# A two-layer gated network behind a normalised attention: chunk 1's second layer by 26 products, transfers of x on one queue, new places for the interleaved steps

## The chip, the cores and the metric

The kernel runs on one core of a Trainium2 chip. The metric is the device time of one execution in microseconds; lower is better. "TensorE", "VectorE", "ScalarE", "GpSimd" and "SyncE" appear in the profile as PE (its weight loads as PEld), DVE, ACT, POOL and SP. A transfer that an engine's queue issues is written SPq, ACTq or POOLq.

## The reference

```python
# q, k, v: (8 batches, 8 heads, 576, 64) float32;  D = 512 = 8 heads x 64
kv  = einsum('bhsd,bhse->bhde', k, v)
out = einsum('bhsd,bhde->bhse', q, kv)
rms = sqrt(mean(out * out, axis=-1, keepdims=True) + 1e-6)
x   = (out / rms * g_norm).transpose(0, 2, 1, 3).reshape(4608, 512)
gate = 1 / (1 + exp(-(x @ w_gate)))      # w_gate, w_val: (512, 1536) float64 in memory
val  = x @ w_val
y    = (gate * val) @ w_out              # w_out: (1536, 512);  y: (4608, 512) float32
```

## The kernel before

The 4608 rows of x are worked in nine chunks of 512 tokens (c = 0 to 8). A chunk has a first layer (x times w_gate and w_val, sigmoid, product: the tensor called h) and a second layer (h times w_out). Batches of 576 rows do not line up with chunks, so x lives in a ring of three chunks (`xT_ring`, tile xT), which batch b+1 fills while chunk b is worked.

Chunk 0 is computed plainly while the weights are converted from float64. From chunk 1 on the first layer is done by a scheme that multiplies matrices cut in 4x2 and 2x4 blocks with 26 products of blocks instead of 32. It runs three times (j = 0, 1, 2, over a third of the hidden units each): 26 products of two 128x256 matmuls. `PRODUCTS1` lists them in order: a PSUM region, the sum of weight blocks, the sum of x blocks, and what is done once the product stands (copies by ScalarE, additions by VectorE, multiplications by GpSimd, sigmoids by ScalarE). The product number p = 26 j + i, 0 to 77, is the clock by which all other steps are placed. `second_layer_fast` does the second layer the same way, with 26 products of three 128x256 matmuls (`PRODUCTS2`). Only five PSUM banks serve the eleven regions: a bank is handed on when its last reader has been issued, so a late VectorE or ScalarE holds up TensorE.

The scheme needs sums of blocks, made by other engines:
- sums of w1 (both first-layer weights, tile w): made once by GpSimd (`w1_sums`, L740), used by chunk 1 where they lie, and stored to memory by SyncE (`keep_w1`, L757, 69 pieces, into kept1) so that chunks 2 to 8 can load them (`load_granule`, L769, on GpSimd's queue);
- sums of x (`x_sums`, 18 a chunk, L829 and L831) by VectorE, placed in the second layer of the chunk before;
- sums of h (`h_sums`, L721), by GpSimd and, for eight of them, by VectorE;
- sums of w_out (18, `W_SUMS`): made once, stored to kept3, and loaded by chunks 2 to 8 (`load_w`, L987).

Chunk 1's second layer is the exception before the change: `second_layer_plain` does it with 4 x 12 matmuls of 128x512, and meanwhile `w_forms` has VectorE make the 18 sums of w_out (L1007, L1009) and GpSimd's queue store them (L1010). Its keep stores of the third part of w1 and four loads of granules fall there too.

Chunks 1 to 6 also carry the attention of batch c + 1 (`feed`). Its steps are: `kv_mm` and four `kv_copies` (L366, L372, L377); two `turn`s for each pair of heads (a VectorE transpose of q, L383, and then the load of the next q by SyncE, L104); and for each two pairs `u_mm` (L407), a square on ScalarE (L413), two sums (L416), a root, two normalisations (L425) and two `x_turn`s. An x_turn has VectorE transpose the result (L432, tile xTs) and then issues the transfers that bring it into the ring (L442): four, or six where the ring wraps. For the first two pairs all are issued by SyncE. For the last two pairs (`two_pairs(n0 + 2, nc.scalar)`) half are issued by ScalarE.

The order of everything is written out by hand: the program runs through the products, and a table says after which product each step is issued. Each engine works its own queue strictly in order. `at1` holds the places in the first layer (p = 0 to 77), `at2` those in the second (0 to 47 matmuls when plain, 0 to 25 products when fast). The last two x_turns are placed at 4 and 8 of the plain layer, and at 4 and 5 of the fast ones. The x sums for the next chunk begin at 23 in the plain layer, at 14 in chunks 2 to 6 and at 6 in chunk 7.

Of the kernel before, what the change touches and what calls it, by code (L numbers as in the profile page):

```python
# [20 lines left out]
def kernel(  # L21
# [332 lines left out]
    def feed(b):  # L354
# [30 lines left out]
            if e == 1:  # L385
                load_q(n + 1)

        def two_pairs(n0, queue=nc.sync):


            d = {}
# [36 lines left out]
            def x_turn(i):  # L428


                for which in range(2):
                    nc.vector.transpose(xTs[:, i, which],  # L432
                                        sq.rearrange("p r (w g i c) -> p w i r g c", w=2, g=JH, i=NC)[:, which, i])
                m = n0 % NHP
                for j in range(2):
                    for e in range(2):
                        p0, p1 = HD * e + QB * j, HD * e + QB * i
                        s0 = 0
                        while s0 < S // 2:
                            o = (S * b + S // 2 * j + s0) % (NX * G)  # L440
                            n_ = min(NX * G - o, S // 2 - s0)
                            (nc.sync, queue)[j].dma_start(out=xT_ring[p1:p1 + QB, m:m + 2, o:o + n_],  # L442
                                                          in_=xTs[p0:p0 + QB, i, :, s0:s0 + n_])
                            s0 += n_

# [3 lines left out]
        def turns_of(n):  # L449
# [2 lines left out]
        n0 = NHP * b  # L452
        kv = [kv_mm] + [lambda i=i: kv_copies(i, range(3)) for i in range(2 * NC)]
        t0, t1, t2, t3 = (turns_of(n0 + i) for i in range(4))
        u0, u1 = two_pairs(n0), two_pairs(n0 + 2, nc.scalar)
        first = list(zip((1, 5, 14, 22, 27, 29, 30, 31, 32, 33, 37, 38, 46, 47, 49, 52, 53, 53, 55, 56, 57, 60, 61, 63),
                         t0 + t1 + u0[:1] + t2[:1] + u0[1:2] + t2[1:] + u0[2:5] + t3[:1] + u0[5:6] + t3[1:] + u0[6:] +
                         u1[:7]))
        return kv, first, u1[7:]

    def flush():
# [73 lines left out]
    def give(i):  # L535
        free.append(i)
# [374 lines left out]
    def first_layer_fast(c, at):  # L911
# [3 lines left out]
        for j in range(N3):  # L915
# [7 lines left out]
            for i, (name, hv, wv, steps) in enumerate(PRODUCTS1):  # L923
                part, p = next(n for n, r in enumerate(PARTS) if i in r), NPR * j + i
                new = name not in regions
                if new:
                    i_ = free.popleft()
                    regions[name] = i_, pair(bank(i_))
                ws = w1_form(c, j, part, hv)
                for g in range(2):  # L930
                    nc.tensor.matmul(regions[name][1][:, g], ws[:, g], xf[c][wv], start=(new and g == 0), stop=True,  # L931
                                     skip_group_check=True)
                combine(o, regions, steps, nc.vector if j == N3 - 1 and i == NPR - 1 else nc.gpsimd)
                give_all(regions, LAST1, i)
                for step in at.get(p, ()):
                    step()
                for _ in range(2 if i % HALF == HALF - 1 else 1):
                    if h_fill:
                        h_fill.popleft()[1]()
                if c > 1:  # L940
                    g_ = NPA * (N3 * (c - 2) + j) + part
                    if p < NPR * N3 - 1:
                        wait = (3 if part < 2 else 0) if j == 0 and c + 1 < B else 0
                        if wait and i == PARTS[part][-1]:
                            held[i + wait] = g_ + NPA
                        elif i == PARTS[part][-1]:
                            load_granule(g_ + NPA)
                        if j == 0 and i in held:
                            load_granule(held.pop(i))
                    k_, r = divmod(p - 20, 2)  # L950
                    if r == 0 and 0 <= k_ < NR:
                        load_w((c - 2) * NS + k_)
                else:
                    if p in (NPR, 2 * NPR):
                        keep_w1(j - 1)
                    if keeping:
                        keeping.popleft()()
                    if NPR <= p < NPR + len(W_ORDER) - W1_FIRST:
                        w1_sums(2, slice(W1_FIRST + p - NPR, W1_FIRST + p - NPR + 1))
                    if p == 2 * NPR + HALF:  # L960
                        load_granule(0)
                        load_granule(1)
            if c > 1:
                h_fill.extend(h_sums(j, slice(SUMS_FIRST) if j else slice(None)))

    tok = [slice(P * i, P * i + P) for i in range(NT)]

# [18 lines left out]
        if i < N_FAST * NS:  # L986
            nc.gpsimd.dma_start(out=ring(i), in_=kept3[i % NS].rearrange("p (j n) -> p j n", j=N3))  # L987

    def w_forms():

        last = {}
        for n, (_, _, x, _, y) in enumerate(W_SUMS):
            last[x] = last[y] = n
        more = h_more.rearrange("p j s c -> p (j s c)").rearrange("p (i j n) -> p i j n", j=N3, n=DH)
        spare = deque(w_ring + [more[:, i] for i in range(2 * N3)])
        at = {v: w_raw(v) for v in range(8)}
        steps = []
        for n, (v, sx_, x, sy, y) in enumerate(W_SUMS):
            at[v] = spare.popleft()
            for u in {x, y, v}:  # L1000
                if u > 7 and last.get(u, n) <= n:
                    spare.append(at[u])

            def make(v=v, sx_=sx_, x=x, sy=sy, y=y, o=at[v], a=at[x], b=at[y]):
                op = op_of(sy)
                if sx_ > 0:
                    tt(out=o, in0=a, in1=b, op=op)  # L1007
                else:
                    nc.vector.scalar_tensor_tensor(out=o, in0=a, scalar=-1.0, in1=b, op0=ALU.mult, op1=op)  # L1009
                nc.gpsimd.dma_start(out=kept3[STREAM.index(v)].rearrange("p (j n) -> p j n", j=N3), in_=o)  # L1010
            steps.append(make)
        return steps

    def second_layer_plain(c, at):
        keep_w1(N3 - 1)
        while keeping:
            keeping.popleft()()
        loads = {4: 2, 8: 3}
        order_ = [block(l, j) for j in range(N3) for l in (0, 2, 1, 3)]
        for t in range(NT):  # L1020
            i = free.popleft()
            ps = bank(i)
            for n, f in enumerate(order_):
                nc.tensor.matmul(ps, gv[c, f][:, tok[t]], w2[:, f, :], start=(n == 0), stop=(n == NFT - 1),
                                 skip_group_check=True)
                if NFT * t + n in loads:
                    load_granule(loads[NFT * t + n])
                for step in at.get(NFT * t + n, ()):
                    step()
            ot = sg_tile()  # L1030
            nc.scalar.copy(out=ot, in_=ps)
            give(i)
            store(c, t, ot)
        load_late(c + 2)

    def second_layer_fast(c, at):
        o = {f"t{n}": temps[:, i, 0:DH] for i, n in enumerate((0, 1, 8, 9))}
# [3 lines left out]
                o[f"o{2 * t + n}"] = rows[t][:, DH * n:DH * n + DH]  # L1041
        regions, used, done = {}, {}, count()
        ends = (nc.sync, nc.scalar) if c == NG - 1 else (nc.sync,)
        dones = {18: 0, 22: 1, 24: 2, 25: 3}

        def product(i, js):
            name, hv, wv, _ = PRODUCTS2[i]
            if i not in used:
                used[i] = name not in regions
                if used[i]:  # L1050
                    regions[name] = take()
            ws = w_raw(wv) if wv < 8 else ring((c - 2) * NS + STREAM.index(wv))
            for j in js:
                nc.tensor.matmul(regions[name][1], h_form(hv, j), ws[:, j], start=(used[i] and j == 0),  # L1054
                                 stop=(j == N3 - 1), skip_group_check=True)
# [1 line left out]
        def finish(i):  # L1057
            _, _, wv, steps = PRODUCTS2[i]
            combine(o, regions, steps, nc.gpsimd)
            give_all(regions, LAST2, i)  # L1060
            if wv > 7 and STREAM.index(wv) + NR < NS:
                load_w((c - 2) * NS + STREAM.index(wv) + NR)
            if i == 16:
                load_granule(NPA * N3 * (c - 1) + NPA - 1)
            if i in dones:
                t = dones[i]
# [50 lines left out]
        store(0, t, ot)  # L1117

    flush()
    for c in range(1, NG):  # L1120
        at1, at2 = {}, {}
        if c + 1 < B:
            kv, first_, then = second_batch if c == 1 else feed(c + 1)
            for p, step in (list(zip((17, 17, 19, 20, 22), kv)) if c > 1 else []) + first_:
                at1.setdefault(p, []).append(step)
            for p, step in zip((4, 8) if c == 1 else (4, 5), then):
                at2.setdefault(p, []).append(step)
        if c + 1 < NG:
            p0, two = (23, 18) if c == 1 else (14, 12) if c + 1 < B else (6, 0)
            p = p0  # L1130
            for n, step in enumerate(lambda n=n, c=c: x_sum(c + 1, n) for n in range(len(X_SUMS))):
                at2.setdefault(p, []).append(step)
                p += (2 if c == 1 else 1) if n % 2 or n >= two else 0
        if c == 1:
            for n, step in enumerate(w_forms()):
                at2.setdefault(2 * n, []).append(step)
        first_layer_fast(c, at1)
        if c == 1:
            sgs += [spare_sg] + more_sgs
        (second_layer_plain if c == 1 else second_layer_fast)(c, at2)  # L1140


# [28 lines left out]
```

## Time and profile before

| what | us |
|---|---|
| median of three runs (1031.4, 1031.47, 1035.5) | 1031.47 |
| profiled execution | 1032.79 |
| span of the profiled execution, first to last instruction | 1031.0 |
| TensorE matmul busy | 1016.1 |
| VectorE busy | 718.1 |
| GpSimd busy | 565.2 |
| ScalarE busy | 347.6 |
| chunk 1: first layer, second layer (plain) | 71.24, 41.20 |
| chunk 6: first layer, second layer (fast) | 74.09, 35.02 |
| chunk 7: first layer, second layer (fast, no batch fed) | 67.53, 33.68 |

The stages are cut where the matmuls change from one line to the other: L931 is the first layer's matmul, L1024 the plain second layer's, L1054 the fast second layer's, L407, L366 and L372 the attention's. A matmul of float32 shows as two records, so a chunk's first layer has 312 records, a fast second layer 156 and the plain one 96. In busy times the clock of TensorE is at its full value throughout (0.999 on average). A group's line gives the count, the busy time, the mean of one in nanoseconds, and the idle time in front of it with what ended that idle time.

### The profile page before, as it was taken

To read this page: it belongs to the slowest core of one execution; us is meant where nothing else is said; L and a number is where in the kernel's file an instruction comes from. 1 tells how busy PE (TensorE), PEld (TensorE's weight loads), DVE (VectorE), ACT (ScalarE), POOL (GpSimd) and SP (SyncE) were. 2 spreads that over 40 slices of the span, in tenths; PEclk is the share of its full clock that TensorE was granted. 3 is DMA by queue.
4 is the path that set the end of the run, shared out by engine and by line. 5 is a ranking of instruction groups with operands and counts; after the bars stand their busy time and mean duration, and the time that the engine had idled before them with its cause. 6 is when DMAs were issued, how large, how long until landed. Compare 5 with 4: busy or idle time off the path is not lost. (4 is left out here: it accounts for less than half of the span.)

```text
span 1031.0 us, 18177 instructions
## 1 busy us (share of the span) xinstructions
PE 1016.1 (99%) x6854; PEld 815.5 (79%) x6854; DVE 718.1 (70%) x1188; ACT 347.6 (34%) x604; POOL 565.2 (55%) x922
## 2 busy tenths in 40 slices
PE   9999999999999999999999999999999999999998
PEld 8644447884588888888888888888888888888887
DVE  4899899776558865786577566866588556755672
ACT  4654422440244304441254115421453033203320
POOL 0001999522149641967087716963396439753963
PEclk9999999999999999999999999999999999999999
DMA  9975311469977466846685567755774656454714
GB/s 263 271 248 171 123 41 53 147 194 305 348 239 251 159 189 221 302 158 194 193 301 179 179 190 254 243 154 170 240 252 159 183 164 240 158 164 154 252 61 121
DMA packets 102183, 203.31 MB, mean 197 GB/s; under 512 B 27792, under 2 KB 74128, under 8 KB 102096
## 3 DMA queue, kind: packets, MB, share of 16 engines
q0 software_dynamic: 24448, 128.20, 37.0%
q1 hardware_dynamic: 68240, 70.08, 23.0%
q10 hardware_dynamic: 9408, 3.87, 1.5%
q8 instruction: 54, 0.88, 0.4%
q14 instruction: 33, 0.27, 0.1%
HBM read 168.30 MB, written 26.74 MB: 189 GB/s over the span
## 5 line engine op out<-in xcount | busy, mean ns | idle before, releaser
L931 PE MATMUL mm<-xs,w 128*128 128x256 f32 x1428 | 334.2, 380 | 0.6 <-DVE h L901 0.4
L931 PEld LDWEIGHTS mm<-xs,w 128*128 128x128 f32 x1428 | 270.0, 190 | 40.7 <-DVE sg L901 1.5
L931 PE MATMUL mm<-xT,w 128*128 128x256 f32 x948 | 230.2, 380 | 0.0
L931 PEld LDWEIGHTS mm<-xT,w 128*128 128x128 f32 x948 | 179.1, 190 | 25.5 <-issue 1.0
L901 DVE TENSOR_TENSOR sg<-sg,mm 128x512 f32<-128x512 f32 (+1 forms) x169 | 98.6, 607 | 112.8 <-PE mm L931 56.8
L769 POOL DMA_DIRECT2D w<-kept x84 | 46.8, 557 | 207.7 <-PE mm L931 199.2
L1054 PE MATMUL mm<-w,h 128*128 128x256 f32 x558 | 126.6, 379 | 0.0
L897 ACT COPY temps<-mm 128x512 f32<-128x512 f32 (+1 forms) x124 | 64.8, 548 | 182.9 <-PE mm L931 92.6
L893 POOL TENSOR_TENSOR h<-h,sg 128x512 f32<-128x512 f32 x72 | 94.1, 1324 | 56.8 <-ACT sg L890 46.4
L1054 PEld LDWEIGHTS mm<-w,h 128*128 128x128 f32 x558 | 106.0, 190 | 14.4
L721 POOL TENSOR_TENSOR h<-h 128x128 f32<-128x128 f32 x189 | 95.3, 516 | 14.5 <-DVE h_more L721 11.4
L890 ACT ACTIVATE sg<-sg 128x512 f32<-128x512 f32 x96 | 59.8, 630 | 107.4 <-DVE sg L901 107.1
L1054 PE MATMUL mm<-w,h_more 128*128 128x256 f32 x390 | 90.1, 380 | 5.6 <-ACT temps L897 5.6
L1054 PEld LDWEIGHTS mm<-w,h_more 128*128 128x128 f32 x390 | 73.7, 190 | 17.5 <-ACT temps L897 7.7
L897 ACT COPY sg<-mm 128x512 f32<-128x512 f32 (+1 forms) x107 | 54.6, 521 | 80.7 <-PE mm L1054 42.7
L560 PE MATMUL mm<-xT,w 128*128 128x512 f32 x176 | 77.7, 594 | 0.0
L901 DVE TENSOR_TENSOR temps<-temps,mm 128x512 f32<-128x512 f32 (+1 forms) x93 | 58.2, 625 | 23.8 <-PE mm L1054 15.6
L901 DVE TENSOR_TENSOR temps<-mm,temps 128x512 f32<-128x512 f32 (+1 forms) x62 | 38.9, 627 | 50.1 <-PE mm L1054 22.5
L897 ACT COPY h<-mm 128x512 f32<-128x512 f32 x48 | 28.0, 585 | 121.9 <-PE mm L931 121.8
L721 POOL TENSOR_TENSOR h_more<-h 128x128 f32<-128x128 f32 x105 | 51.9, 497 | 30.7 <-DVE h L893 27.3
L740 POOL TENSOR_TENSOR h_more<-w 128x256 f32<-128x256 f32 x10 | 12.9, 1302 | 97.5 <-PE at L366 97.5
L987 POOL DMA_DIRECT2D w<-kept x102 | 62.8, 617 | 1.4 <-issue 1.0
(140 smaller groups left out, 1347.7 us busy)
## 6 DMA issues: line engine op xcount, KB each, us to landing
w<-kept POOLq DMA_DIRECT2D x102, 384.0 KB, 4.8
w<-kept POOLq DMA_DIRECT2D x42, 896.0 KB, 5.4
w<-kept POOLq DMA_DIRECT2D x42, 768.0 KB, 5.3
w_ring<-kept POOLq DMA_DIRECT2D x24, 384.0 KB, 5.0
q<-in_q_dram SPq DMA_DIRECT2D x24, 288.0 KB, 3.7
out_dram<-sg SPq DMA_DIRECT2D x104, 64.0 KB, 1.7
st<-in_moe_w_gate_dram SPq DMA_DIRECT2D x12, 512.0 KB, 5.4
st<-in_moe_w_val_dram SPq DMA_DIRECT2D x12, 512.0 KB, 6.7
```

The lines of the kernel that those rows point to most:

```text
L560: nc.tensor.matmul(self.ps[i], w[("wg", "wv")[i], self.f][:, m, :], xT[self.c][:, m, :], start=(m == 0), stop=(m == NMT - 1), skip_group_c ...
L721: ops.append((eng, lambda v=v, x=x, sign=sign, y=y, eng=eng: eng.tensor_tensor(out=h_form(v, j), in0=h_form(x, j), in1=h_form(y, j), op=op ...
L740: nc.gpsimd.tensor_tensor(out=w1_slot(j, w_at[v]), in0=w1_slot(j, w_at[x]), in1=w1_slot(j, w_at[y]), op=op_of(sign))
L769: nc.gpsimd.dma_start(out=granule(g)[:, 0:n], in_=kept1[g // NPA % N3, g % NPA][:, 0:n])
L890: nc.scalar.activation(out=o["o" + step[1]], in_=o["o" + step[1]], func=AF.Sigmoid)
L893: mult.tensor_tensor(out=o[x], in0=o[x], in1=o[y], op=ALU.mult)
L897: nc.scalar.copy(out=o[out_], in_=o[expr])
L901: tt(out=o[out_], in0=o[x], in1=o[y], op=ALU.add if sign == "+" else ALU.subtract)
L931: nc.tensor.matmul(regions[name][1][:, g], ws[:, g], xf[c][wv], start=(new and g == 0), stop=True, skip_group_check=True)
L987: nc.gpsimd.dma_start(out=ring(i), in_=kept3[i % NS].rearrange("p (j n) -> p j n", j=N3))
L1054: nc.tensor.matmul(regions[name][1], h_form(hv, j), ws[:, j], start=(used[i] and j == 0), stop=(j == N3 - 1), skip_group_check=True)
```

## The change

1. **Chunk 1's second layer** is done by `second_layer_fast` like the others; `second_layer_plain` and `w_forms` go. The 18 sums of w_out are made one by one by `w_form` (L999, L1001 in the new file): nine in chunk 1's first layer and nine in its second layer, each at a place in the table, 12 by VectorE and 6 by GpSimd (the number at the end of each triple says which: 1 is GpSimd). They lie in parts of w1 that are already used and stored (`w_place`, `W_AT`). Each is stored to kept3 by SyncE instead of GpSimd's queue.
2. **Keep stores of w1** start at p = 0 instead of 26, one after each product; those of the third part start at p = 39. The four granule loads for chunk 2 move to products 9, 10, 13 and 23 of the second layer. Sums of h are now made in chunk 1 too.
3. **All transfers of x** are issued by SyncE.
4. **Places**: the attention's steps, the k-by-v steps and the x sums get new places in chunks 1 to 7, as explicit lists, with one list for the steps of batch 2 (chunk 1) and one for the other batches.

The diff, cut to its core:

```diff
-        def two_pairs(n0, queue=nc.sync):
+        def two_pairs(n0):
...
-                            (nc.sync, queue)[j].dma_start(out=xT_ring[p1:p1 + QB, m:m + 2, o:o + n_],
+                            nc.sync.dma_start(out=xT_ring[p1:p1 + QB, m:m + 2, o:o + n_],
...
-        u0, u1 = two_pairs(n0), two_pairs(n0 + 2, nc.scalar)
-        first = list(zip((1, 5, 14, 22, 27, 29, 30, 31, 32, 33, 37, 38, 46, 47, 49, 52, 53, 53, 55, 56, 57, 60, 61, 63),
-                         t0 + t1 + u0[:1] + t2[:1] + u0[1:2] + t2[1:] + u0[2:5] + t3[:1] + u0[5:6] + t3[1:] + u0[6:] +
-                         u1[:7]))
+        u0, u1 = two_pairs(n0), two_pairs(n0 + 2)
+        steps_ = t0 + t1 + t2 + t3 + u0 + u1[:7]
+        first = [(p, steps_[i]) for p, i in (((4, 0), (5, 1), (8, 2), (21, 3), (25, 8), (28, 4), (28, 5), (29, 9), (30, 10), (31, 11), (32, 6), (42, 12), (48, 13), (48, 7), (50, 14), (53, 15), (53, 16), (53, 17), (56, 18), (57, 19), (57, 20), (60, 21), (60, 22), (65, 23)) if b == 2 else
+                                             ((3, 0), (7, 1), (24, 2), (24, 3), (28, 8), (28, 4), (30, 5), (30, 9), (32, 10), (32, 11), (37, 12), (39, 6), (45, 13), (47, 7), (47, 14), (53, 15), (53, 16), (54, 17), (56, 18), (56, 19), (56, 20), (60, 21), (61, 22), (63, 23)))]
...
-                    if p in (NPR, 2 * NPR):
-                        keep_w1(j - 1)
+                    if p == 0:
+                        keep_w1(0)
+                        keep_w1(1)
+                    elif p == NPR + HALF:
+                        keep_w1(2)
...
-                    if p == 2 * NPR + HALF:
-                        load_granule(0)
-                        load_granule(1)
-            if c > 1:
-                h_fill.extend(h_sums(j, slice(SUMS_FIRST) if j else slice(None)))
+            h_fill.extend(h_sums(j, slice(SUMS_FIRST) if j else slice(None)))
...
+    def w_place(at):
+        return w1_flat[:, at:at + N3 * DH].rearrange("p (j n) -> p j n", j=N3)
+
+    W_AT = {v: w_place(at) for v, at in {10: 0, 12: 768, 14: 1536, 9: 2304, 13: 3072, 16: 4096, 19: 4864, 11: 5632, 8: 6400}.items()}
+    W_AT.update((v, w_raw(v)) for v in range(8))
+    W_AT.update(zip((22, 20, 21, 17, 18, 25, 23), w_ring[:5] + w_ring[6:]))
+    W_AT.update(((24, w_raw(5)), (15, w_raw(0))))
+
+    def w_form(v, eng):
+        sx_, x, sy, y = next(s_[1:] for s_ in W_SUMS if s_[0] == v)
+        if sx_ > 0:
+            eng.tensor_tensor(out=W_AT[v], in0=W_AT[x], in1=W_AT[y], op=op_of(sy))
+        else:
+            nc.vector.scalar_tensor_tensor(out=W_AT[v], in0=W_AT[x], scalar=-1.0, in1=W_AT[y], op0=ALU.mult,
+                                           op1=op_of(sy))
+        nc.sync.dma_start(out=kept3[STREAM.index(v)].rearrange("p (j n) -> p j n", j=N3), in_=W_AT[v])
...
+        first_loads = {9: 0, 10: 1, 13: 2, 23: 3}
...
-            ws = w_raw(wv) if wv < 8 else ring((c - 2) * NS + STREAM.index(wv))
+            ws = W_AT[wv] if c == 1 else w_raw(wv) if wv < 8 else ring((c - 2) * NS + STREAM.index(wv))
...
+    X1 = (12, 15, 16, 18, 18, 18, 18, 19, 19, 20, 20, 21, 21, 22, 22, 23, 23, 23)
+    X2 = (14, 15, 16, 17, 19, 19, 22, 23, 24, 25, 25, 25, 25, 25, 25, 25, 25, 25)
+    X3 = (7, 8, 11, 11, 12, 13, 14, 14, 16, 16, 19, 22, 22, 22, 22, 23, 23, 23)
...
-            for p, step in (list(zip((17, 17, 19, 20, 22), kv)) if c > 1 else []) + first_:
+            for p, step in (list(zip((19, 19, 19, 24, 24), kv)) if c > 1 else []) + first_:
...
-            for p, step in zip((4, 8) if c == 1 else (4, 5), then):
+            for p, step in zip((4, 4) if c == 1 else (5, 5), then):
...
-            p0, two = (23, 18) if c == 1 else (14, 12) if c + 1 < B else (6, 0)
...
+            for n, p in enumerate(X1 if c == 1 else X2 if c + 1 < B else X3):
+                at2.setdefault(p, []).append(lambda n=n, c=c: x_sum(c + 1, n))
...
+            for at_, forms in ((at1, ((27, 9, 0), (28, 10, 0), (34, 12, 0), (52, 8, 1), (53, 13, 0), (56, 14, 0), (62, 11, 1), (71, 16, 1), (74, 19, 0))), (at2, ((0, 22, 0), (3, 23, 1), (4, 25, 1), (6, 21, 1), (8, 24, 0), (9, 15, 0), (10, 20, 0), (12, 17, 0), (12, 18, 0)))):
...
-        (second_layer_plain if c == 1 else second_layer_fast)(c, at2)
+        second_layer_fast(c, at2)
```

## The prediction

> **What bounds it now.** I read the page first, then the busy time by stage, the chain of waits, the waits in total and the timeline of one second layer.
>
> ```profile
> PE 1016.1 (99%) x6854; PEld 815.5 (79%) x6854; DVE 718.1 (70%) x1188; ACT 347.6 (34%) x604; POOL 565.2 (55%) x922
> L1024 PE MATMUL mm<-w,h 128*128 128x512 f32 x96 | 41.4, 592 | 0.0
> ```
>
> TensorE is never short of work for long, so only two things can shorten the kernel: fewer matmul columns, or the few stalls left. The stages from 162 us on (cut where the matmuls change line):
>
> ```profile
> 162.38:233.62 71.24, 71.24 (x601) 62.49 (x600) 55.94 (x89) 30.65 (x48) 39.39 (x45) 1.00 0.45 143
> 233.62:274.82 41.20, 41.20 (x97) 18.24 (x96) 27.51 (x47) 1.66 (x3) 10.88 (x20) 1.00 0.94 340
> ...
> 788.77:823.79 35.02, 33.93 (x157) 29.56 (x156) 23.21 (x56) 3.35 (x9) 18.88 (x39) 1.00 0.49 145
> ...
> 891.32:925.00 33.68, 33.68 (x158) 29.65 (x157) 23.20 (x53) 3.35 (x9) 20.17 (x39) 1.00 0.51 152
> ```
>
> Columns: length, then busy time of PE, PEld, DVE, ACT, POOL, then clock, DMA share, GB/s. Row 1 is chunk 1's first layer, row 2 its plain second layer (41.20 us, DMA at 340 GB/s), row 3 chunk 6's second layer by 26 products, row 4 the same for chunk 7, which feeds no batch. The work is 33.68 us; chunk 6 loses 1.34 us. The chain says where:
>
> ```profile
> 796.34 0.76 DVE xTs L432 x2
> 797.10 0.02 issue
> 797.12 0.64 ACTq L442
> 797.76 0.04 issue
> 797.80 0.82 ACTq L442
> 798.62 0.04 issue
> 798.66 0.38 ACT temps L897
> 799.04 0.04 issue
> 799.09 24.87 PE mm L1054 x114
> ```
>
> ScalarE stands in its queue behind two transfers of x (L442), which wait for VectorE's transposes (L432); the copy of product 4's sum (L897) comes late, and product 7, which accumulates into that bank, waits. Behind 799 the chain is TensorE alone. It recurs once in each of chunks 2 to 6:
>
> ```profile
> PE mm L1054 <- ACT temps L897: 5.6, 5, 1.3
> SPq L442 <- DMA xT<-xTs: 6.8, 4, 3.1
> ```
>
> Line 1: 5.6 us in five waits. Line 2: SyncE's transfers of x also wait for earlier ones to land (used below).
>
> [...] The trace agrees: SP and ACT issue L442 in 0.60 and 0.64 us, landing after 4.6 and 5.1 us. Moving the issue should cost SP's time alone. [...] The trace fits: the x sums (L829, 128x256) take 421 ns at the median and 950 ns at most, the long ones at 161 to 168 us beside GpSimd's L740. [...] GpSimd's rows agree: (1324 - 497) / 384 = 2.15 ns (L893 128x512 against L721 128x128).
>
> **Part 1: chunk 1's second layer.** Removed: 96 matmul records of 128x512, 41.20 us. Added: 26 products, 156 records, 33.68 us by chunk 7's row. TensorE's work: **-7.5 us**. The copies, combinations and sums of h that come with the 26 products are those of chunk 7's row (DVE 23.2, POOL 20.2, ACT 3.4 us busy), where they hide behind TensorE. What may stall it:
>
> (a) Sums of w_out. VectorE makes 12 (6 in each layer), GpSimd 6 (3 in each). VectorE's take 0.95 us each (L1007 rows): 5.7 us on top of 23.2 busy in a second layer of 33.7, so 29 of 34, and tight. GpSimd's 128x768 has no row: by the slope, 0.50 + 640 x 2.15 ns = 1.9 us; at worst three times L740's locked 1.42 us, 4.3 us; I take 1.9. GpSimd's sum 25 is needed soonest, by product 11, which starts 11 x 1.296 = 14.3 us into the layer. In chunk 6 GpSimd's first eight sums of h end near 8.4 us, 7.8 without the 0.6 us load issued between them; then sum 23, two of h, sum 25: 7.8 + 1.9 + 1.0 + 1.9 = 12.6 us. Hidden by 1.7 us at my price; at 4.3 us it would cost TensorE 3.1. The 18 stores of the sums leave GpSimd's queue (L1010, 0.54 us each, 9.8 us) for SP's; GpSimd is not the bound, so I count nothing for that.
>
> (b) x for chunk 2. The two transposing steps run behind VectorE's eight sums of h and form 22, at about 8.4 to 10 us. SP then issues 12 transfers, and ahead of them stands the store of GpSimd's sum 23 (ready at 9.7). SP and ACT have eight completion counters in rotation: a transfer waits for the one eight before. Twelve at 0.63 us from 10.2: the eleventh, the last chunk 2 needs, goes out at 16.5 us and lands after 3 us in quiet (first layer of chunk 1: 212.29 to 215.04) or 6 to 9 as in the old plain layer: 19.5 to 25. VectorE reaches its first x sum at about 18.2 us and stands in order, with two sums of w_out and the subtraction that frees product 18's bank behind it: 19.9 + 1.9 + 0.4 = 22.2 us against 23.3 needed; four operations later product 19's bank, 24.4 against 24.6. So there is next to no slack, and GpSimd's locks cost some. I charge **1.4 us** (0 to 5).
>
> (c) First layer of chunk 1 (0.1 us of stall visible now): six VectorE sums, 5.7 us over 56 of 71 busy, three by GpSimd (39 of 71 busy). Stores of w1 go out earlier, from product 0, one a product; each landed in 1.9 us, and the first sum placed over them comes five products behind the last. If the sum of product 52 on GpSimd is late, SP's queue with x behind it is late too, with some 3 us to spare. **+0.4 us** (0 to 2). The granule loads, now at products 9, 10, 13 and 23, are first read 20 us on: nothing, covered by the rest of the layer.
>
> **Part 2: transfers of x by SyncE.** In chunks 2 to 6 ACT no longer waits. The five second layers sum to 175.33 us; five times 33.68 is 168.4: 6.9 us to gain. What is late next: VectorE's o1=o1+B at 798.10 needs only to precede product 11, and GpSimd's sums end 5 us or more ahead of their products. SP issues 8 transfers instead of 4 (12 in the wrapped chunk): 797.12 + 7 x 0.63 = 801.5, landed by 807, against the first x sum at about 809. Hidden, with 2 us to spare; without that cover each late microsecond would stand in front of VectorE's combinations. Behind them on SP are only the stores of the output, 10 us later. I take **-6.5 us** (-7 to -3).
>
> **Part 3: places of steps.** First layers of chunks 2 to 6 sum to 373.6 us. Their work is 67.5 (chunk 7) + 5.9 (72-head block twice 1.78 and 1.73, k by v 2.41) + 0.3 for switching = 73.75; the excess is 4.9. Of it 1.2 us is a wait with no releaser (549.28), which no step touches. Visible causes: in chunk 3 VectorE held 3.86 us by a q load that the turn at product 14 reached too soon (0.57 us of TensorE), and k-by-v copies late for the matmul at product 27 (0.3). The new places (turns at 24, matmul at 28) clear both; copies on ACT now bunch at 24. **-1.0 us** (-2.5 to +2). The nine x sums put at product 25 run into the next first layer, where VectorE's first combination is due 6 us in; nine take 3.8: nothing, covered by that gap.
>
> **Sum.** -7.5 + 1.4 + 0.4 - 6.5 - 1.0 = **-13.2 us**. The profiled execution took 1032.79 us (span 1031.0, 1.8 around it), the median of the runs is 1031.47. Against the profiled one it gives 1019.6 (span near 1018); against the median, 1018.3, which I forecast.
>
> **Rivals.**
> 1. *The handover from chunk 1 becomes the wait.* SP has 18 stores of w_out and 69 of w1 in one queue with x. For: the old layer's x landed in 6 to 9 us, and (b) has no slack. Against: that was beside 340 GB/s, now spread. TensorE would lose 4 to 9 us there: 1022 to 1027.
> 2. *The ACT wait is replaced* in chunks 2 to 6 by one of similar size, for VectorE's bank releases or SP. For: PE comes 1.3 us earlier to VectorE. Against: VectorE idles 2.16 and 0.94 us right after. Part 2 then brings 0: 1024.8.
> 3. *Slower.* x by SyncE alone lands late in all of chunks 1 to 6: each x sum blocks VectorE, and TensorE stops for a bank. It decides once landing takes 2 us over chunk 6's 5; at 10 us each chunk loses 3 to 4: six give about 20, no 6.5 gain, less 7.5: about 1037. For: eight in flight at most. Against: 8 transfers need no second round, and nothing landed so late outside the saturated layer.
> 4. *It doesn't do what it says*: product 11 or others wait for their sums and chunk 1's layer stays near 41 us: 1024.
>
> **Numbers.** As forecast (1014.5 to 1022): 0.72. Rivals 1, 2 and 4 together 0.24, four fifths of it under 1026.3. Rival 3: 0.04. 0.5%, 5.2 us, is about what a measurement of this kernel can tell from no change: faster 0.89, same 0.07, slower 0.04. The range holds the forecast's own spread and the larger part of rivals 1, 2 and 4: 1014 to 1025.5.
>
> **What would show it.** Right: chunk 1's second layer at 34 to 36 us with 156 records of 128x256; the wait of L1054 on ACT gone and chunks 2 to 6 at 33.7 to 34.2; no L442 on ACT. Wrong: VectorE waiting for xT in the x sums (rival 1, 3), TensorE waiting for VectorE in L1054 (2), or for GpSimd's sums (4), or first layers of chunks 2 to 6 above 74.7 us on average.

## The result and the profile after

| | before | after |
|---|---|---|
| median of four runs each, us | 1031.93 (1031.4 to 1035.5) | 1020.83 (1019.7 to 1023.12) |
| profiled execution, its span | 1032.79, 1031.0 | 1021.93, 1020.1 |

The ratio is 0.9888 with a 95% interval from 0.9858 to 0.9918: faster by 1.1%, where the forecast of 1018.3 us, 2.5 us too low, meant 1.3%. The page of the kernel after (busy time of each engine with its share and instruction count; then the group of second-layer matmuls):

```profile
span 1020.1 us, 18402 instructions
...
PE 1008.7 (99%) x6914; PEld 828.8 (81%) x6914; DVE 730.1 (72%) x1211; ACT 349.5 (34%) x609; POOL 614.5 (60%) x986
...
L1024 PE MATMUL mm<-w,h 128*128 128x256 f32 x636 | 144.7, 379 | 0.9 <-POOL h L721 0.8
```

TensorE is 7.4 us less busy, GpSimd 49 us more: it now makes chunk 1's sums of h and six of the sums of w_out. The second layer's matmul, L1024 in the new file, has only the 128x256 form left. Its idle time is no longer ScalarE's doing but, once, GpSimd's.

The stages of the kernel after, cut as before (columns: length, busy time of PE, PEld, DVE, ACT, POOL, granted clock, DMA share, GB/s). The rows are chunk 1's first and second layer, chunk 2's first and second layer, chunk 6's and chunk 7's second layer:

```profile
162.66:235.37 72.71, 71.69 (x601) 62.33 (x600) 64.96 (x94) 30.11 (x47) 69.44 (x91) 1.00 0.54 181
235.37:270.77 35.40, 34.47 (x158) 29.35 (x157) 32.90 (x64) 3.98 (x10) 27.65 (x38) 1.00 0.78 269
270.77:348.87 78.10, 75.97 (x681) 65.95 (x680) 51.79 (x84) 34.55 (x59) 45.81 (x76) 0.98 0.74 252
348.87:382.54 33.67, 33.67 (x157) 29.64 (x156) 20.37 (x48) 3.35 (x9) 19.60 (x39) 1.00 0.54 159
780.53:814.20 33.67, 33.67 (x158) 29.64 (x157) 20.45 (x48) 3.35 (x9) 18.56 (x39) 1.00 0.50 151
881.54:915.21 33.67, 33.67 (x158) 29.64 (x157) 23.03 (x53) 3.35 (x9) 20.28 (x39) 1.00 0.47 147
```

No transfer of x is left on ScalarE; SyncE's land after 4.5 us at the median (issues, KB, us to landing):

```profile
xT<-xTs SPq DMA_DIRECT2D x80, 72.0 KB, 4.5
```

Chunk 6's second layer (row 5 of the stages) is now as long as chunk 7's (row 6), and both equal TensorE's busy time. Chunk 1's (row 2) fell from 41.20 to 35.40. But row 1 grew by 1.5 us, with GpSimd busy in 69.44 of 72.71 us, and row 3, chunk 2's first layer, took 78.10 instead of 74.49, at a mean clock of 0.98. Set against the steps of the prediction, stage by stage from the two profiled executions:

| stage | forecast, us | measured, us |
|---|---|---|
| chunk 1's first layer | +0.4 | +1.48 |
| chunk 1's second layer | -6.1 | -5.81 |
| chunk 2's first layer | part of -1.0 | +3.62 |
| first layers of chunks 3 to 6 | part of -1.0 | -2.18 |
| second layers of chunks 2 to 6 | -6.5 | -6.98 |
| start, chunks 7 and 8, end | 0 | -1.0 |
| sum | -13.2 | -10.9 |

Nearly all of the missing gain lies in chunk 2's first layer, where the forecast had no cost at all. What TensorE and others waited for between 210 and 300 us (total, times, longest, us):

```profile
PE at L366 <- DMA h_more<-in_v_dram: 2.1, 2, 1.7
...
PEld at L366 <- DMA h_more<-in_k_dram: 1.8, 1, 1.8
ACT sg L897 <- POOL h L893: 1.7, 1, 1.7
...
PEld mm L931 <- ACT sg L897: 1.4, 1, 1.4
...
PEld mm L1024 <- POOL h L721: 1.2, 1, 1.2
...
DVE xs L829 <- DMA xT<-xTs: 0.4, 1, 0.4
```

These are three losses. At 217.7 us TensorE loses 1.2 us, because a copy by ScalarE (L897) comes behind GpSimd's multiplication (L893). At 260.4 us product 18 waits 0.94 us for GpSimd's sum of h (L721); a shorter wait, 0.32 us for VectorE, lies just before it. At 288.1 us the k-by-v matmuls (L366) find k and v not loaded: the block takes 5.37 us instead of 2.41, so 2.96 are lost. x, which the prediction had feared, costs VectorE 0.4 us. The chain of waits (start, length, what) names the third loss too:

```profile
256.93 1.13 POOL h_more L721
258.06 1.13 POOL h L721
259.19 0.65 POOL w L769
...
259.85 0.66 POOL h_more L721
...
260.59 0.53 POOL h L721
...
261.17 9.76 PE mm L1024 x44
270.93 11.98 PE mm L931 x56
282.91 9.05 DMA h_more<-in_v_dram
291.95 0.14 issue
292.09 0.84 PE at L366 x16
```

Up to 261 the chain is GpSimd's queue; then TensorE runs unhindered to 282.9; then one load of v takes 9.05 us. After this stall TensorE's clock stood at half for 3.413 us (from 292.5 us on), worth another 1.1 us by an estimate: 78.11 less the 74.01 of a chunk 2 without the stall (e2 below) less 2.96. Not every execution has that stretch: two of the four had a mean granted clock of 1.000, which leaves no room for it, and took 1019.7 us.

### The profile page after: what moved, and what is told of

The parts are those of the page before. It is cut to its first block, busy times and chain, and to the rows that moved or that the text cites. A ratio compares the mean times of both kernels' runs of the same rounds, so it can differ in the third digit from the quotient of the medians.

```text
span 1020.1 us, 18402 instructions
## 1 busy us (share of the span) xinstructions
PE 1008.7 (99%) x6914; PEld 828.8 (81%) x6914; DVE 730.1 (72%) x1211; ACT 349.5 (34%) x609; POOL 614.5 (60%) x986
## 4 chain that ended last, share of the span: by engine, by line
PE 72%; POOL 2%; DMA 1%; DVE 1%; issue 0%; ACT 0%; POOLq 0%; DVEq 0%
PE mm L931 45%; PE mm L1024 24%; PE at L407 2%; POOL h L721 1%; DMA h_more<-in_v_dram 1%; PE at L366 1%; DVE sg L901 0%; POOL h_more L721 0%; POOL w_ring L999 0%; PE at L372 0%; POOL w L999 0%; DVE h L901 0%; DVE sqs L425 0%; POOL w L769 0%; ACT sg L897 0%
## 5 line engine op out<-in xcount | busy, mean ns | idle before, releaser
L901 DVE TENSOR_TENSOR sg<-sg,mm 128x512 f32<-128x512 f32 (+1 forms) x176 | 101.1, 598 | 88.3 <-PE mm L931 51.5
L769 POOL DMA_DIRECT2D w<-kept x84 | 46.9, 558 | 181.2 <-PE mm L931 179.7
L1024 PE MATMUL mm<-w,h 128*128 128x256 f32 x636 | 144.7, 379 | 0.9 <-POOL h L721 0.8
L1024 PEld LDWEIGHTS mm<-w,h 128*128 128x128 f32 x636 | 120.6, 190 | 18.1 <-POOL h L721 1.2
L897 ACT COPY temps<-mm 128x512 f32<-128x512 f32 (+1 forms) x128 | 66.1, 537 | 191.4 <-PE mm L931 96.2
L893 POOL TENSOR_TENSOR h<-h,sg 128x512 f32<-128x512 f32 x72 | 98.5, 1385 | 46.1 <-ACT sg L890 34.5
L721 POOL TENSOR_TENSOR h<-h 128x128 f32<-128x128 f32 x216 | 114.2, 541 | 16.7 <-DVE h_more L721 13.1
L1024 PE MATMUL mm<-w,h_more 128*128 128x256 f32 x456 | 104.1, 379 | 0.0
L1024 PEld LDWEIGHTS mm<-w,h_more 128*128 128x128 f32 x456 | 86.6, 190 | 12.1 <-DVE h L901 0.4
L897 ACT COPY sg<-mm 128x512 f32<-128x512 f32 (+1 forms) x112 | 57.1, 510 | 90.3 <-PE mm L1024 48.1
L721 POOL TENSOR_TENSOR h_more<-h 128x128 f32<-128x128 f32 x120 | 57.2, 480 | 34.0 <-DVE h L893 30.1
L740 POOL TENSOR_TENSOR h_more<-w 128x256 f32<-128x256 f32 x10 | 12.8, 1298 | 97.8 <-PE at L366 97.8
L897 ACT COPY h<-mm 128x512 f32<-128x512 f32 x48 | 28.0, 584 | 127.5 <-PE mm L931 124.3
L901 DVE TENSOR_TENSOR sg<-mm,sg 128x512 f32<-128x512 f32 (+1 forms) x64 | 39.5, 617 | 42.7 <-PE mm L1024 21.7
```

The lines of the kernel that those rows point to most:

```text
L721: ops.append((eng, lambda v=v, x=x, sign=sign, y=y, eng=eng: eng.tensor_tensor(out=h_form(v, j), in0=h_form(x, j), in1=h_form(y, j), op=op ...
L740: nc.gpsimd.tensor_tensor(out=w1_slot(j, w_at[v]), in0=w1_slot(j, w_at[x]), in1=w1_slot(j, w_at[y]), op=op_of(sign))
L769: nc.gpsimd.dma_start(out=granule(g)[:, 0:n], in_=kept1[g // NPA % N3, g % NPA][:, 0:n])
L893: mult.tensor_tensor(out=o[x], in0=o[x], in1=o[y], op=ALU.mult)
L897: nc.scalar.copy(out=o[out_], in_=o[expr])
L901: tt(out=o[out_], in0=o[x], in1=o[y], op=ALU.add if sign == "+" else ALU.subtract)
```

## The experiments

The theory: the gain is the sum of two independent parts (chunk 1's second layer; ScalarE freed in chunks 2 to 6), and the missing 2.5 us are the price of what chunk 1 now packs into GpSimd and the DMA. "c1" and so on stand for chunks; lengths are of the profiled execution; a ratio is to the kernel before, timed beside the run, with its 95% interval.

**e1: before, with all transfers of x by SyncE.** Nothing else of the change.

```diff
-        u0, u1 = two_pairs(n0), two_pairs(n0 + 2, nc.scalar)
+        u0, u1 = two_pairs(n0), two_pairs(n0 + 2)
```

> The kernel before, with only the transfers of x moved to SyncE (places unchanged). Theory (ScalarE's queue held the copy of product 4's sum): the second layers of chunks 2 to 6 go from 35.0 to 33.7 us each, 6.9 us in all, the wait of L1054 on ScalarE is gone; total 1025. Rival (the new places did it, or SP takes over as the wait): the second layers stay at 34.5 or more, total 1029 or more.

Measured: 1030.42 us (20 runs) beside 1034.2, ratio 0.997 [0.9955, 0.9984]. The second layers of c2 to c6 are all 33.67 us, c1's stays at 41.20. So the queue alone takes ScalarE's wait away, 7.0 us in the five layers. Yet the whole gained less, 3 us by the ratio. The profiled execution (1028.05 us) shows one reason: c4's first layer took 77.71 us with two waits that have no releaser.

```profile
PE at L407 <- issue: 3.4, 2, 2.9
```

They lie inside an attention block that no edit touched. Before has one such wait too, 1.1 us in the same chunk, and after one of 0.9 us in c3 (415 us); the last section says what they have in common. Without them the first layers of c3 to c6 sum to 296.9 us here and to 296.1 in after. So the new places of the first layers are worth some 0.8 us, an estimate from two single executions.

**e2: after, with half of the last pairs' transfers on ScalarE again.**

```diff
...
-        u0, u1 = two_pairs(n0), two_pairs(n0 + 2)
+        u0, u1 = two_pairs(n0), two_pairs(n0 + 2, nc.scalar)
```

> The changed kernel with half of the last two pairs' transfers of x given back to ScalarE. Theory: the five second layers return to about 35.0 us, +6.9 us, total about 1027.7; chunk 1's second layer gains a wait of the same kind. Rival (the new places keep ScalarE's queue clear of it): under +2 us.

Measured: 1024.9 us, ratio 0.9917 [0.9889, 0.9944]. In c2 to c6 nothing came back: 33.67 us in each. But c1's second layer went from 35.4 to 42.6. ScalarE's waits there, between 236 and 262 us:

```profile
ACT temps L897 <- DMA xT<-xTs: 7.6, 1, 7.6
...
PE mm L1024 <- ACT temps L897: 5.9, 1, 5.9
```

ScalarE issues its transfers (eight of the twelve here) one after the other from 244.58 to 249.93 us, and the copy that TensorE needs stands behind them (249.98). So the 7.6 us are for the most part its own issuing, though the view names a landing. TensorE loses 6.02 us, and from 248.8 us on, still within the stall, its clock stands at half for 6.83 us.

**e8: e2, and one of the two steps that start those transfers at product 4 again.** This asks why e2 lost nothing in c2 to c6.

```diff
-            for p, step in zip((4, 4) if c == 1 else (5, 5), then):
+            for p, step in zip((4, 4) if c == 1 else (4, 5), then):
```

> The kernel e2 (after with half of the last pairs' x on ScalarE again), with the first of the two steps that start those transfers at product 4 of the second layers of chunks 2 to 6, as before has it, instead of product 5. Theory (in these chunks the later place was a second cure of ScalarE's wait, beside the queue): their second layers go back to some 35.0 us each. Rival (the place of this step is not what keeps ScalarE clear; what is queued ahead is): they stay at 33.7 us. Chunk 1's second layer keeps e2's 42.6 us either way.

Measured: 1031.4 us (one run); c2 to c6 are back at 35.02, 35.23, 35.02, 35.02 and 35.02 us. Its chain in c6 is that of the kernel before, piece for piece:

```profile
796.22 0.76 DVE xTs L432 x2
...
797.00 0.64 ACTq L442
...
797.68 0.81 ACTq L442
...
798.54 0.38 ACT temps L897
...
798.96 24.87 PE mm L1024 x114
```

So in c2 to c6 there were two cures, and either suffices: the queue at the old places (e1), or one product later on the old queue (e2). In c1 SyncE is needed.

**e3: after, with chunk 2's k-by-v steps later.** The steps that need them in the same layer follow.

```diff
-            for p, step in (list(zip((19, 19, 19, 24, 24), kv)) if c > 1 else []) + first_:
+            kv_at = (24, 24, 24, 26, 26) if c == 2 else (19, 19, 19, 24, 24)
+            for p, step in (list(zip(kv_at, kv)) if c > 1 else []) + first_:
...
-(28, 8), (28, 4), (30, 5), (30, 9), (32, 10), (32, 11)      # for b == 3 only
+(31, 8), (31, 4), (32, 5), (33, 9), (34, 10), (34, 11)
```

> The changed kernel with chunk 2's k-by-v matmul at product 24 instead of 19 (its copies at 24 and 26, u_mm and what hangs on it at 31 to 34). Theory (k and v land at about 292 us, 4 us after TensorE asks for them; TensorE stands 3 us and then runs 3.4 us at half clock): the first layer of chunk 2 goes from 78.1 to 74 us, no half-clock stretch before the end, total about 1016.5. Rival (the lost 4 us are DMA congestion that stalls other things as well): the layer stays above 76 us, with waits elsewhere.

Measured: 1018.2 us, ratio 0.986 [0.9829, 0.989]. c2's first layer:

```profile
270.70:345.50 74.80, 74.09 (x682) 64.57 (x681) 50.88 (x84) 34.70 (x59) 46.38 (x76) 1.00 0.77 260
```

74.80 us instead of 78.11, at full clock: nearer to the theory's 74 than to the rival's 76 and more. (The time of the whole doesn't show the gain: the interval overlaps after's.) The loads landed no earlier (291.58 us); TensorE just asked later, at 292.38. A stall of 0.87 us is new at 299 us, behind ScalarE's copies of k by v, now close to the next users.

**e5: after, with two of chunk 2's granule loads later.** Is the DMA crowded by them?

```diff
-        first_loads = {9: 0, 10: 1, 13: 2, 23: 3}
+        first_loads = {9: 0, 10: 1, 23: 2}
...
+                if c == 2 and p == 6:
+                    load_granule(3)
```

> The changed kernel with chunk 2's third granule loaded at product 23 instead of 13 of chunk 1's second layer and the fourth at product 6 of chunk 2's first layer instead of 23. Theory (the four granules, 3.3 MB, fill the DMA engines from 259 to 277 us and delay output stores, and k and v behind them on SP): k and v land 3 us or more earlier, the k-by-v wait falls from 3 us to under 0.5, the first layer of chunk 2 to about 74 us, total 1016.5. Rival (SP's order and counters delay k and v, whatever the granules do): the wait stays at 2 to 3 us, total 1020.

Measured: 1022.45 us, ratio 0.9891 [0.986, 0.9923]. The last load landed 20.3 us into c2's first layer instead of 21.2, where 3 us and more were expected. The k-by-v block lost 1.72 us instead of 2.96 and no half clock followed, so that layer took 75.75 us. The whole doesn't show it: in the profiled execution, which has a half-clock stretch near its start, chunk 1's first layer began 4.0 us later than in after. The granules are part of the cause, no more. The trace of after points to SyncE's order for the rest. Its queue's own waits in after, between 265 and 285 us:

```profile
SPq L495 <- DMA h_more<-in_v_dram: 5.3, 2, 5.0
```

The stores of the output (L495) stand ahead of k and v (L118) on SP, and one of them waits 5.0 us for a load that ScalarE had issued to land. By the semaphores of the trace, the transfers of SyncE and ScalarE share eight completion counters in turn; the store's turn came to the counter which that load held (landed at 276.38 us, store issued at 276.39). k and v leave SP only from 278.15 us on, 7.4 us into the layer; before, they left at 276.97, 2.2 us into it. Then they share the DMA: from 255 to 290 us it is 93% busy at 328 GB/s, and a granule takes 9 us to land. Such a crowd is not new, though: before, from 261 to 290 us, the DMA was 96% busy at 342 GB/s. Set against before, the last load of v leaves 1.5 us later and takes 9.0 us to land instead of 6.9. No run changed SyncE's order, so its share is read from the trace and not shown.

What a kernel loses at this place is the landing of the last of k and v against the moment when TensorE reaches them:

| kernel | last landing, us | L366 reached, us | lost, us |
|---|---|---|---|
| before | 288.31 | 290.84 | 0 |
| after | 291.95 | 288.13 | 2.96 |
| e3 | 291.58 | 292.38 | 0 |
| e5 | 295.22 | 292.23 | 1.72 |
| e6 | 290.37 | 288.88 | 0.23 |
| e7 | 287.60 | 290.74 | 0 |
| e12 | 290.36 | 287.16 | 1.92 |

The change moved the landing 3.6 us later and TensorE 2.7 us earlier: a margin of 2.5 us became a deficit of 3.8, of which the block hides some, as the last load is not read at once.

**e6: after, with no sum of h started at products 26 to 33 of c1's first layer.** This takes on the two GpSimd waits.

```diff
-                for _ in range(2 if i % HALF == HALF - 1 else 1):
+                for _ in range(0 if c == 1 and NPR <= p < NPR + 8 else 2 if i % HALF == HALF - 1 else 1):
```

> After, but in chunk 1's first layer no sum of h is started at products 26 to 33, so that GpSimd has less queued when it must make the part of h that the sg copy at 217 us waits for; the sums left over come later, in the rest of the first layer and in the second. Theory (GpSimd's queue was late because the sums of h stand ahead of L893's part): the 1.2 us stall of TensorE at 217 us goes and chunk 1's first layer takes 71.5 us instead of 72.7; the second layer stays at 35.4. Rival (the lateness lies in the sums of w_out or in L740, which stay where they are): the stall stays at 1.0 us or more. Second rival (the sums postponed are late for the second layer): the first layer gains 1.2 us and the second layer's wait for GpSimd grows by as much or more.

Measured: 1022.26 us (1018.38 to 1024.24), ratio 0.9888 [0.9858, 0.9919], the same as after. Its c1 layers:

```profile
162.32:233.65 71.33, 71.33 (x601) 62.40 (x600) 64.85 (x93) 30.15 (x47) 65.25 (x85) 1.00 0.55 186
233.65:271.52 37.87, 34.75 (x158) 29.31 (x157) 33.88 (x65) 3.99 (x10) 33.53 (x45) 1.00 0.74 259
```

The stall at 217 us is gone (71.33 us, all of it TensorE), so its cause was GpSimd's queue. But GpSimd's work has only slipped on: 4.2 us less of it in the first layer, 5.9 us more in the second (33.53 us busy, from 27.65), which takes 37.87 us with three stalls for GpSimd. That is the second rival. The two layers together lose 1.1 us by it. Pacing moves the lateness; it doesn't remove it.

**e7: after, without three of GpSimd's sums of w_out in c1's second layer.**

```diff
-        if sx_ > 0:
+        if v in (21, 23, 25):
+            pass
+        elif sx_ > 0:
```

> After, with the three sums of w_out that GpSimd makes in chunk 1's second layer (products 21, 23 and 25) left out: nothing is computed for them, and the products read what lies there, so this part of the output is not the reference's. Theory (product 18 waits 1.26 us because GpSimd's sums of h stand behind the sums of w_out of 1.8 us each): the wait goes and chunk 1's second layer takes 34.1 us instead of 35.4. Rival (VectorE, or the landing of x, holds product 18): the wait stays within 0.3 us, and so does the layer.

Measured: 1021.41 us (one run). Neither number came. c1's second layer took 38.2 us, longer than with the sums (some of it at half clock, from 262.0 us on); product 18 no longer waits for GpSimd but for VectorE (2.37 us), and VectorE for x. Its tile xT from 244 to 262 us (the transfers, who waited for whom, and the time to landing):

```profile
L442 SPq DMA_DIRECT2D xT<-xTs x12: 585/595/1166, 244.8 to 252.7; - x12
...
  DVE xs L829: 4.6, 1
...
DMA to landing us min/median/max: 1.8/2.4/6.3
```

The last transfers take 6.3 us to land, where after's longest took 3.3. With less in front of them, GpSimd had started the first two granule loads at 251.7 and 253.6 us, ahead of after's 259.1 and 261.1.

**e12: e7, with the granule loads behind the last transfer of x.** If that is why x was late, it must now be on time.

```diff
-        first_loads = {9: 0, 10: 1, 13: 2, 23: 3}
+        first_loads = {14: 0, 15: 1, 16: 2, 23: 3}
```

> The kernel e7 (three sums of w_out of GpSimd in chunk 1's second layer left out, so that part of the output is not the reference's), with chunk 2's first three granule loads moved from products 9, 10 and 13 to products 14, 15 and 16, where GpSimd starts them after the last transfer of x has been issued. Theory (in e7 it was the granule loads, started at 251.7 and 253.6 us, that made the last transfers of x land at 258.3 us and TensorE lose 2.4 us): the last x lands within 2.5 us of its issue, at 256 us or earlier, and chunk 1's second layer takes 34.0 us instead of 38.2. Rival (x is late for another reason, such as the stores of the sums of w_out on the same queue): x lands later than 257 us and the layer takes 36 us or more.

Measured: 1019.27 us (one run).

```profile
235.87:269.81 33.94, 33.94 (x158) 29.52 (x157) 29.80 (x64) 3.98 (x10) 20.88 (x35) 1.00 0.80 276
```

c1's second layer takes 33.94 us, with no stall. The last x lands at 255.75 us, 1.9 us after its issue. Both halves are shown: GpSimd's sums hold product 18 in after, and that same lateness keeps the granules out of x's way. The 1.5 us between after's layer and this one are what GpSimd's lateness costs there.

**e10: e3 and e6 together.**

> The edits of e3 and e6 together: k and v of chunk 2 used later, and no sum of h started at products 26 to 33 of chunk 1's first layer. Theory: the two stalls are independent, so chunk 1's first layer takes 71.5 us and chunk 2's 74.8 us, and the time is some 1017 us, 4 us under after (a ratio to before of .985 to .986). Rival (the postponed sums make the second layer of chunk 1 later): chunk 1's second layer takes 36.5 us or more and the time stays at e3's 1018.2 us.

Measured: 1020.34 us, ratio 0.987 [0.9847, 0.9893], which can't be told from e3. c1 took 71.34 and 37.62 us, as in e6: its rival again. c2's first layer took 76.57, with two stalls of 0.9 and 1.2 us at 301 and 317 us. The trace names ScalarE's copy (L898) for the first, as in e3, and VectorE's addition (L902) for the second; why that addition is late stays open.

**e11: e3, with three sums of h paced and one sum of w_out moved from GpSimd to VectorE.**

```diff
-                for _ in range(2 if i % HALF == HALF - 1 else 1):
+                for _ in range(0 if c == 1 and 30 <= p <= 32 else 2 if i % HALF == HALF - 1 else 1):
...
-(62, 11, 1)
+(62, 11, 0)
```

> The kernel e3 with two edits in chunk 1's first layer: no sum of h is started at products 30 to 32, and the sum of w_out that GpSimd made at product 62 (1.8 us) is made by VectorE, which stands idle for some 3 us between 217 and 226 us. Theory (GpSimd's queue is what holds both layers of chunk 1, and delaying sums as in e6 only moves the lateness on, while taking 1.8 us of work away cures both waits): first layer 71.4 us (from 72.7), second layer 34.3 us at most (from 35.5), chunk 2's first layer 74.8 us as in e3, time some 1015.6 us. Rival (a GpSimd that is ready earlier starts the granule loads of chunk 2 earlier, as in e7, and these delay the last transfers of x): the first layer gains, but the second layer takes 36 us or more, with VectorE waiting for x.

Measured: 1018.74 us beside 1034.74, ratio 0.9849 [0.9829, 0.9868]. The first layer came to 71.24 us as expected, the second to 35.94, with a wait of 1.39 us for GpSimd's sum of h. x was on time, so the rival did not happen either. The two layers together gained 1.1 us on e3, of the 2.5 expected: what TensorE gained in the first layer brought it to product 18 that much sooner, and GpSimd was again the later. c3's first layer lost 2.0 us to a wait without a releaser (410 us), so the profiled span, 1017.0 us, is no shorter than e3's 1016.1. This is the lowest ratio of all kernels here, but it can't be told from e3's 0.986. Its interval and after's overlap by 0.001; the two were not timed in one comparison, so how far it beats after stays an estimate, some 4 us.

## Why the prediction was right, and where not

**Part 1, the work: right.** The layer's 156 records of 128x256 ran at chunk 7's rate: in e12, with nothing in the way, it takes 33.94 us.

**Part 1 (a): right in the main.** GpSimd's sums of 128x768 took 1.8 us each, priced at 1.9; VectorE's took 1.1 to 2.0 us, 1.36 on average, where 0.95 was the price. Sum 25 was ready 13.6 us into the layer, forecast 12.6, needed at 14.3. No product waited for its weights, and rival 4 fell.

**Part 1 (b): the size right, the cause another.** The layer lost 1.7 us, I charged 1.4. But the charge was for x, and x was on time: the eleventh transfer landed 20.3 us into the layer (forecast 19.5 to 25), and VectorE waited 0.4 us. What stopped product 18 was GpSimd's sums of h. I had followed its queue only up to sum 25, under "GpSimd is not the bound", and of "GpSimd's locks" (b) says that they "cost some", without a number. No run shows a lock; what the traces show is that operations of the two engines take longer beside each other. In before an x sum (L829) took 410 to 427 ns with no GpSimd operation beside it, and 674 ns at the median, 950 at most, with one; L740 took 716 to 731 ns alone and 907 at the median, 2215 at most, beside VectorE. In after's layer six of these sums of h took 1.05 to 1.18 us, each of them while VectorE made a sum of w_out of 128x768, where 0.45 is usual; and GpSimd's own three sums of w_out stand among them. In e7 the mechanism I had described did occur, with x landing 23 us in and 2.4 us lost. So the warning of no slack was right, and it was luck of the order that GpSimd stopped TensorE first.

**Part 1 (c): failed in size, +1.48 us against +0.4.** I set three sums of w_out on 39 us of GpSimd's work and left out that the sums of h are now made in that layer as well, 43 of them before 235 us. GpSimd came to 69.4 of 72.7 us. An engine that seemed to have 32 us to spare was in fact full.

**The granule loads, "nothing, covered by the rest of the layer": failed, and this is the largest miss.** I asked when the granules are first read. The question was what else is in flight while they load. k and v of the next batch, for whose landing the prediction has no term, share the DMA with them and stand on SP behind the output's stores. The shorter second layer also brings every deadline behind it nearer to loads whose start depends on other things: chunk 2 began 4.1 us earlier, and by the margin table TensorE reached k and v 2.7 us earlier while they landed 3.6 us later. The price was 3.0 us of stall and, in the profiled execution, 1.1 at half clock. That the stall is a matter of this margin is shown (e3); that the granules make k and v late is shown for a part of it (e5).

**Part 2: right, -6.98 us against -6.5.** Rivals 2 and 3 did not happen: the second layers of chunks 2 to 6 are at TensorE's own time. Rival 1, x late at the handover from chunk 1, shows in e7 alone. (Rival 3's sum does not come out: 1031.5 + 20 - 7.5 is 1044, not 1037.) But the cause is not the queue alone. The step of part 4 of the change that moves the transposes from products 4 and 5 to 5 and 5, which I had not priced in the second layers, would have done it by itself (e2, e8). Where SyncE is indispensable is chunk 1, worth 7.2 us there (e2), which I had not separated out. Before the change this could not show, since ScalarE has only three operations in the plain layer.

**Part 3: -1.0 us forecast, some 0.8 us by an estimate.** Chunks 3 to 6 gained 2.2 us. Without the wait that has no releaser in each of the two (1.1 us in before, 0.9 in after) it would be 2.0, of which e1 gets 1.2 without new places. Of before's wait the prediction says that "no step touches" it; in fact after has it in another chunk, and shorter. In chunk 2 the new places did no harm of their own: the k-by-v matmuls went from product 17 to 19, and the wait was for the loads.

**The sum** thus came out 2.3 us short: chunk 2's first layer (+3.6) and chunk 1's (+1.1 beyond its charge) went against it; the other first layers, the second layers of chunks 2 to 6 and the ends of the kernel gave some back.

## What to carry to other kernels

When a stage is shortened, move every later deadline forward by the gain and compare it with the landing of what is loaded there: a landing set by another queue need not move along (here TensorE came 2.7 us earlier and k and v landed 3.6 us later). Before calling an engine free, count all the work that the edit gives it in the very stage, and price its operations as they run beside the engines that will run beside them (GpSimd's sums of h: up to 1.18 us beside VectorE's sums of w_out, where 0.45 is usual). A late engine may be shielding a transfer (in e7 GpSimd, ready earlier, started two loads some 7 us sooner, and the longest landing of x went from 3.3 to 6.3 us), so after curing one wait look at what the cured engine now starts earlier.

## What the hardware showed that was not expected

**Half clock after windows that are idle in part.** The half-clock stretches within the kernel last 3.413 us (after, e5, e7) or twice that (e2, e8), and in each of these five executions the stretch at the kernel's end begins a whole multiple of 3.413 us after the first one (213, 293, 222, 227 and 229 times). So a grid of windows of 3.413 us can be laid over each execution. On that grid, TensorE's matmuls were idle for 62% (after), 63% (e1, at its end), 65% (e5, e7) or more of the window before a half-clock stretch. At full clock, the idlest windows that none followed have 54% (e11) and 50% (e1, e12). So in these executions the length of a stall doesn't decide alone: 2.2 us of idle time inside one window came before the half clock (e7), while 2.9 us did not, cut by the window's edge into 35% and 50% of two (e1). The grid lies elsewhere in each execution (the first half clock begins at 292.5 us in after, 262.0 in e7 and 248.8 in e2, no whole number of windows apart). That this is why two executions of after have no such stretch is a guess that no run tests.

**Waits with no releaser.** TensorE stood idle for 2.9 us before one attention matmul in e1, for 1.1 us in before and for 1.8 us in a first layer in e11, with no releaser in the profile. The DMA records show what these waits share. The instruction queue (q8) brings packets of 16 KB, 55 in after: 65 bytes for each of TensorE's 13828 records, so they look like its program. In all twelve runs, between 160 and 1000 us, each of the 14 gaps of 0.15 us and more that the profile puts down to "issue" ended 1.3 to 1.6 us after such a packet had landed, though only one comes every 18 us or so. That TensorE had run out of instructions there is the author's guess; no run isolates it. The places are not chance either: after and seven of the runs built on it have such a gap, of 0.2 to 1.8 us, 32 us into chunk 3's first layer, while before and e1 have theirs in chunk 4. At up to 2.9 us they are as large as the edits studied, so a stage's length should be compared without them.
